# Attention block on one core: loads in cycles of 16 units, the remainder rows of P transposed by DMA

## The chip, the cores and the metric

The kernel runs on one core of a Trainium2 chip. Its time is the device time of that core in microseconds (us), the median over executions. The core has a matrix engine (TensorE, PE in the profile, with its weight loads shown apart as PEld), a vector engine (DVE), a scalar engine (ACT), GpSimd (POOL) and SyncE (SP), which computes nothing and issues transfers. Each engine works through its own list of instructions in order; semaphores tie the lists together. Sixteen DMA engines move the data.

## What is computed

Two independent attention blocks, A and B, have the same shapes: 16 batches, 144 query rows, model width 448, 16 heads, 512 keys, head width 256, all in bf16. K and V come from a cache. Each block is

```python
q = (x @ wq).reshape(B, Sq, H, Dh).transpose(0, 2, 1, 3)
scores = einsum("bhqd,bhkd->bhqk", q, k_cache) * (Dh ** -0.5)
p = softmax(scores, axis=-1)
o = einsum("bhqk,bhkd->bhqd", p, v_cache)
out = o.transpose(0, 2, 1, 3).reshape(B, Sq, H * Dh) @ wo
```

and the output joins A's and B's along the last axis.

## The kernel before

A **unit** U is one head of one batch: 256 units for A, then 256 for B. One Python loop over a step number i writes out the work of all engines in order; at step i it emits stages of several units at once, so that each engine always has work of some unit. `LQ`, `LS`, `LT` and `LSB` say how many steps a stage runs ahead of the step in which the unit's last stage, PV, is emitted.

- **Q** (L314, unit i+15): 8 matmuls project x of the unit's batch into one PSUM bank; `t_evac_q` (L326 on DVE or L330 on ACT) copies the result, scaled, to `qt_sb`.
- **SA** (L418, unit i+5): scores of the first 112 query rows, 2 matmuls of 512 columns into one of two banks. DVE takes the row maxima (L429), ACT the exponentials and their sums (L440), DVE the reciprocal (L450), POOL multiplies (L458, `t_norm`). The reciprocal and the multiplication of unit i+4 are emitted in step i, behind the maximum of unit i+5.
- **TA** (L471, unit i+2): four TensorE transposes of that P into the same bank; DVE copies them to `pt_sb` (L481).
- **SB, TB**: the remaining 32 query rows of four units share one set of 128 partitions. Every eighth step SB (L342) makes these scores for eight units in two banks; L354, L364, L374 and L382 do the softmax as above; TB (L394, four TensorE transposes for a group G of four units) and a DVE copy (L403, `t_evac_ptb`) bring them into the last 32 columns of `pt_sb`. TB stands between TA and PV in its step.
- **PV** (L504, unit i): 8 matmuls of V with the transposed P; ACT copies the result to `ring` (L519, L521).
- **OP** (L542): the product with wo, for chunks of 128 output rows, in pieces of two matmuls of 448 columns. A credit that grows by `OP_RATE` a step says how many pieces a step takes; a step takes none, one, two or more pairs. L560 evacuates a chunk, L571 stores it, issued on POOL.

A small planner (`_Sched`) puts in the semaphore waits: an instruction waits for the last writers of what it reads and the last readers of what it overwrites, and for nothing else.

SP issues the loads, in the order of `dma_plan`. K comes for eight units at a time through a transposing DMA of 2 MB (L290, three buffers), V for four units in a plain 1 MB copy (L299, three buffers), x for four batches in two transposing DMAs (L280, L281), the weights wq and wo as plain copies (L259, L261, L269). The list is sorted by the step in which the data is needed, so that a K and two V's alternate. A load whose buffer is still being read makes SP wait, and all later loads with it.

Of the kernel before, what the change touches and what calls it, by code (L numbers as in the profile page):

```python
# [122 lines left out]
def bass_concat_heads__mha_block_cached__gqa_block_cached__near_ridge_kernel(  # L123
# [37 lines left out]
    LQ, LS, LT = 15, 5, 2  # L161
    LSB = 7
    NK, NV, NXG = 3, 3, 3
    XB = 4 if Bn % 4 == 0 else (2 if Bn % 2 == 0 else 1)
    NQT, NPA, NPB, NPT, NST, NSTB, NOST = 12, 5, 2, 8, 4, 2, 3
# [9 lines left out]
    with contextlib.ExitStack() as es:  # L175
# [9 lines left out]
        kt_sb = sb("kt_sb", [128, NK, 2, 8 * SK], BF16)  # L185
# [4 lines left out]
        pb_sb = sb("pb_sb", [128, NPB, SK], BF16)  # L190
        pt_sb = sb("pt_sb", [128, NPT, 4, SQ], BF16)
        ost_sb = sb("ost_sb", [128, NOST, D], BF16)
        ident = sb("ident", [128, 128], BF16)
        ones = sb("ones", [128, 128], BF16)
# [7 lines left out]
        ptb_ps = [t.bitcast(BF16) for t in sb_ps]  # L202
# [3 lines left out]
        for i in range(NK):  # L206
            sem_names.append("kt%d" % i)
        for i in range(NV):
            sem_names.append("v%d" % i)
        for i in range(NXG):  # L210
            sem_names.append("xt%d" % i)
        for i in range(HG):
            sem_names.append("wq%d" % i)
        for i in range(NWG):
            sem_names.append("wo%d" % i)
        for i in range(NOST):
            sem_names.append("ost%d" % i)
        sems = {n: es.enter_context(nc.semaphore("s_" + n)) for n in sem_names}
# [10 lines left out]
        def t_ident():  # L229
            def e1(g):  # L230
                return g.memset(ones[:], 1.0)
            S.add(POOL, e1, writes=[("ones", 0)], name="ones")

            def e2(g):
                return g.affine_select(ident[:], ones[:], pattern=[[1, 128]], compare_op=ALU.is_equal,
                                       fill=0.0, base=0, channel_multiplier=-1)
            S.add(POOL, e2, reads=[("ones", 0)], writes=[("ident", 0)], name="ident")
# [36 lines left out]
        def t_load_x(XG):  # L274
            pr, j = divmod(XG, Bn // XB)
            sl = XG % NXG
            x = xs[pr][j * XB:(j + 1) * XB].rearrange("b q d -> (b q) d")

            def e(q):
                q.dma_start_transpose(xt_sb[:, sl, 0:3, :], x[:, 0:384]).then_inc(sems["xt%d" % sl], 16)  # L280
                return q.dma_start_transpose(xt_sb[:, sl, 3, :], x[:, 320:448]).then_inc(sems["xt%d" % sl], 16)  # L281
            S.add(SP, e, writes=[(("xt", sl), XG)], dma_sem="xt%d" % sl, n_dma=2, name="x%d" % XG)

        def t_load_k(SG):
            pr, r0 = divmod(8 * SG, NU)
            sl = SG % NK
            src = ks[pr].rearrange("b h k d -> (b h k) d")[r0 * SK:(r0 + 8) * SK, :]

            def e(q):
                return q.dma_start_transpose(kt_sb[:, sl, :, :], src).then_inc(sems["kt%d" % sl], 16)  # L290
            S.add(SP, e, writes=[(("kt", sl), SG)], dma_sem="kt%d" % sl, name="k%d" % SG)

# [9 lines left out]
        def t_q(U):  # L302
# [15 lines left out]
            S.add(PE, e, reads=[(("wq", hg), pr), ("wqz", 0), (("xt", xsl), XG)], writes=[("qp", ("q", U))],  # L318
                  banks=["qp"], name="Q%d" % U)

        def t_evac_q(U):
            sl = U % NQT
            src = qp_ps[:, 0:2 * SQ].rearrange("p (c q) -> p c q", c=2)
            if (U - LQ) % 8 in (2, 4, 6, 7):
# [8 lines left out]
        def t_sb(SG):  # L333
            ksl = SG % NK

            def e(t):
                ins = None
                for dc in range(2):
                    for jj in range(8):
# [3 lines left out]
                                       rhs=kt_sb[:, ksl, dc, jj * SK:(jj + 1) * SK], start=(dc == 0), stop=(dc == 1),  # L343
                                       tile_position=(0, 32 * j))
                return ins
            S.add(PE, e, reads=[(("qt", (8 * SG + jj) % NQT), 8 * SG + jj) for jj in range(8)] + [(("kt", ksl), SG)],
# [12 lines left out]
        def t_exp_b(G):  # L359
            sl = G % NSTB  # L360
            psl = G % NPB

            def e(a):
                return a.activation(pb_sb[:, psl, :], sb_ps[G % 2][:, :], AF.Exp,  # L364
# [3 lines left out]
                  writes=[(("pb", psl), (G, 0)), (("rsumb", sl), G)], banks=["sb%d" % (G % 2)], name="exb%d" % G)  # L368
# [8 lines left out]
        def t_norm_b(G):  # L377
            sl = G % NSTB
            psl = G % NPB

            def e(g):
                return g.tensor_tensor(pb_sb[:, psl, :], pb_sb[:, psl, :],  # L382
                                       stat[:, RINVB + sl:RINVB + sl + 1].to_broadcast([128, SK]), op=ALU.mult)
            S.add(POOL, e, reads=[(("pb", psl), (G, 0)), (("rinvb", sl), G)], writes=[(("pb", psl), (G, 1))],
                  name="nmb%d" % G)

        def t_tb(G):
            psl = G % NPB

            def e(t):  # L390
                src = pb_sb[:, psl, :].rearrange("q (p c) -> q c p", c=4)
                ins = None
                for c in range(4):
                    ins = t.transpose(ptb_ps[G % 2][:, c * 128:(c + 1) * 128], src[:, c, :], ident[:, :])  # L394
                return ins
            S.add(PE, e, reads=[(("pb", psl), (G, 1)), ("ident", 0)], writes=[(("sbb", G % 2), ("t", G))],
                  banks=["sb%d" % (G % 2)], name="TB%d" % G)

        def t_evac_ptb(G):
            s0 = (4 * G) % NPT  # L400

            def e(v):
                return v.tensor_copy(pt_sb[:, s0:s0 + 4, :, QA:SQ],  # L403
                                     ptb_ps[G % 2][:, 0:512].rearrange("p (c j q) -> p j c q", c=4, j=4))
            S.add(DVE, e, reads=[(("sbb", G % 2), ("t", G))],
                  writes=[(("ptb", (4 * G + j) % NPT), 4 * G + j) for j in range(4)], banks=["sb%d" % (G % 2)],
                  name="eptb%d" % G)

        def t_sa(U):
            SG = U // 8  # L410
            ksl = SG % NK
            bank = U % 2
            ko = (U % 8) * SK
# [7 lines left out]
            S.add(PE, e, reads=[(("qt", U % NQT), U), (("kt", ksl), SG)], writes=[(("sap", bank), ("s", U))],  # L421
# [144 lines left out]
        def t_store(r):  # L566
# [6 lines left out]
            S.add(POOL, e, reads=[(("ost", sl), r)], dma_sem="ost%d" % sl, name="st%d" % r)  # L573
# [4 lines left out]
        t_ident()  # L578
        dma_plan = []

        def plan(lo, deadline, lead, fn, *args):
            dma_plan.append((deadline, len(dma_plan), lo, lead, fn, args))

        s_min = -LQ - 24
        for XG in range(NXGT):
            pr, j = divmod(XG, Bn // XB)
            u_first = pr * NU + j * XB * H
            dl = u_first - LQ
            if XG >= NXG:
                pr0, j0 = divmod(XG - NXG, Bn // XB)  # L590
                lo = pr0 * NU + (j0 + 1) * XB * H - 1 - LQ + 1
            else:
                lo = s_min
            plan(lo, dl, 40, t_load_x, XG)
        for pr in range(NP):
            for hg in range(HG):
                dl = pr * NU + 4 * hg - LQ
                lo = pr * NU - H + 4 * hg + 3 - LQ + 1 if pr > 0 else s_min
                plan(lo, dl, 10 ** 6, t_load_wq, pr, hg)
        for wg in range(NWG):  # L600
            plan(s_min, H - 4 + 2 * wg, 10 ** 6, t_load_wo, 0, wg)
        for SG in range(NSG):
            dl = 8 * SG - LSB
            lo = 8 * (SG - NK) + 7 - LS + 1 if SG >= NK else s_min
            plan(lo, dl, 12, t_load_k, SG)
        for G in range(NG):
# [194 lines left out]
```

## Time and profile before

| what | us |
|---|---|
| median of 3 runs (lowest to highest) | 1213.86 (1212.51 to 1214.36) |
| span of the profiled execution | 1210.9 |
| DVE busy | 770.1 |
| ACT busy | 753.9 |
| POOL busy | 679.6 |
| TB, L394 MATMUL, 512 of them, busy | 49.8 |
| DVE copies behind TB, L403, 128 of them, busy | 53.0 |
| POOL multiplications L458 and L382, 640 of them, busy | 665.8 |
| store issues on POOL, L571, 36 of them, busy | 21.0 |

The span goes from the first to the last instruction of one profiled execution; a timed run holds some 3 us more. Busy time of PE is the sum of modelled matmul durations, and matmuls overlap, so PE's load is better read from the distance between the starts of matmuls of neighbouring steps. DMA moved 243 GB/s on the mean over the span.

### The profile page before, as it was taken

The numbers are of one execution on the slowest core, as the hardware profiler recorded it, in microseconds if no ns is written. First come the engines' busy times: TensorE is split into PE (matmuls) and PEld (weight loads), VectorE is DVE, ScalarE is ACT, GpSimd is POOL, SyncE is SP. The second block draws the span as 40 slices with busy tenths as digits, with TensorE's granted clock in tenths as the row PEclk, the third lists the DMA queues.
The fourth block names the chain that finished last, engine by engine and source line by source line (L and its number), as shares of the span: only waits on it lengthen the run. The fifth ranks groups of instructions, "written<-read, shape, count | busy, mean of one in ns | idle before, by whom it ended". The sixth has DMA issues, their size and how long they took to land.

```text
span 1210.9 us, 33868 instructions
## 1 busy us (share of the span) xinstructions
PE 1176.6 (97%) x13952; PEld 902.6 (75%) x13952; DVE 770.1 (64%) x2179; ACT 753.9 (62%) x2213; POOL 679.6 (56%) x682
## 2 busy tenths in 40 slices
PE   4998999999999999999999999999999999999997
PEld 3676777777777777777777777777877777777765
DVE  1765666666666666666566666666666666666563
ACT  1655666666666666666566666666666666666553
POOL 0654565565555565565555655655655655655553
PEclk9999999999999999999999999999999999999999
DMA  9999999999999999999999999999999999999971
GB/s 250 296 269 290 246 255 225 242 251 246 245 238 234 228 263 231 239 239 233 278 284 272 278 272 267 247 257 224 245 245 236 226 245 244 244 239 243 223 178 47
DMA packets 627033, 294.15 MB, mean 243 GB/s; under 512 B 548416, under 2 KB 556608, under 8 KB 626880
## 3 DMA queue, kind: packets, MB, share of 16 engines
q1 hardware_dynamic: 625152, 287.85, 102.2%
q0 software_dynamic: 1728, 4.13, 1.2%
q8 instruction: 111, 1.82, 0.6%
q14 instruction: 42, 0.34, 0.1%
HBM read 148.90 MB, written 4.13 MB: 126 GB/s over the span
## 4 chain that ended last, share of the span: by engine, by line
PE 90%; DMA 6%; DVE 2%; SPq 1%; ACT 0%; issue 0%; POOL 0%; ACTq 0%
PE qp_ps L314 20%; PE ot_ps L504 19%; PE sa_ps L418 18%; PE op_ps L542 17%; PE sa_ps L471 8%; PE sb_ps L342 5%; DMA kt_sb<-in_A_k_cache_dram 4%; PE sb_ps L394 2%; DMA kt_sb<-in_B_k_cache_dram 1%; DVE stat L429 1%; DMA wq_sb<-in_A_wq_dram 0%; PE qp_ps L542 0%; SPq L280 0%; DVE qt_sb L326 0%; DVE pt_sb L481 0%
## 5 line engine op out<-in xcount | busy, mean ns | idle before, releaser
L458 POOL TENSOR_TENSOR pa_sb<-pa_sb,stat 112x512 bf16<-112x512 bf16 x512 | 532.7, 1041 | 491.6 <-DVE stat L450 491.4
L440 ACT ACTIVATE pa_sb<-sa_ps,stat 112x512 bf16<-112x512 f32 x512 | 352.0, 688 | 409.6 <-DVE stat L429 408.6
L429 DVE TENSOR_REDUCE stat<-sa_ps 112x1 f32<-112x512 f32 x512 | 353.9, 691 | 324.7 <-PE sa_ps L418 321.4
L314 PEld LDWEIGHTS qp_ps<-xt_sb,wq_sb 128*128 128x128 bf16 x4096 | 290.5, 99 | 93.1 <-issue 11.3
L314 PE MATMUL qp_ps<-xt_sb,wq_sb 128*128 128x144 bf16 x4096 | 344.1, 228 | 16.1 <-DMA wq_sb<-in_A_wq_dram 10.3
L504 PE MATMUL ot_ps<-pt_sb,v_sb 128*128 128x144 bf16 x4096 | 340.9, 226 | 0.0
L418 PE MATMUL sa_ps<-kt_sb,qt_sb 128*112 128x512 bf16 x1024 | 311.1, 385 | 1.0 <-DVE pt_sb L481 0.8
L542 PE MATMUL op_ps<-wo_sb,ring 128*128 128x448 bf16 x1120 | 279.6, 353 | 0.0
L504 PEld LDWEIGHTS ot_ps<-pt_sb,v_sb 128*128 128x128 bf16 x4096 | 269.1, 98 | 0.4
L471 PEld LDWEIGHTS sa_ps<-ident,pa_sb 112*128 112x128 bf16 x2048 | 161.2, 114 | 104.9 <-ACT pa_sb L440 24.8
L519 ACT ACTIVATE ring<-ot_ps 128x288 bf16<-128x288 f32 (+8 forms) x512 | 190.3, 372 | 4.5 <-PE ot_ps L504 4.5
L481 DVE COPY pt_sb<-sa_ps 128x448 bf16<-128x448 bf16 x512 | 190.5, 372 | 2.4 <-PE sa_ps L471 2.4
L471 PE MATMUL sa_ps<-ident,pa_sb 112*128 112x112 bf16 x2048 | 186.5, 213 | 0.1
L326 DVE TENSOR_SCALAR qt_sb<-qp_ps 128x288 bf16<-128x288 f32 x256 | 117.0, 457 | 98.2 <-PE qp_ps L314 97.5
L382 POOL TENSOR_TENSOR pb_sb<-pb_sb,stat 128x512 bf16<-128x512 bf16 x128 | 133.1, 1040 | 27.1 <-DVE stat L374 27.1
L330 ACT ACTIVATE qt_sb<-qp_ps 128x288 bf16<-128x288 f32 x256 | 106.0, 414 | 35.1 <-PE qp_ps L314 33.4
L418 PEld LDWEIGHTS sa_ps<-kt_sb,qt_sb 128*112 128x112 bf16 x1024 | 96.9, 129 | 38.5 <-issue 26.8
L542 PEld LDWEIGHTS op_ps<-wo_sb,ring 128*128 128x128 bf16 x1120 | 95.5, 98 | 28.1 <-issue 0.9
L440 ACT ACTIVATION_READ_ACCUMULATOR pa_sb<-sa_ps,stat 112x1 f32 x512 | 98.9, 193 | 0.0
L354 DVE TENSOR_REDUCE stat<-sb_ps 128x1 f32<-128x512 f32 x128 | 87.1, 680 | 3.6 <-PE sb_ps L342 3.6
L364 ACT ACTIVATE pb_sb<-sb_ps,stat 128x512 bf16<-128x512 f32 x128 | 88.5, 691 | 0.0
L450 DVE RECIPROCAL stat<-stat 112x1 f32<-112x1 f32 x512 | 78.4, 153 | 0.5 <-ACT pa_sb L440 0.5
(23 smaller groups left out, 368.4 us busy)
## 6 DMA issues: line engine op xcount, KB each, us to landing
v_sb<-in_A_v_cache_dram SPq DMA_DIRECT2D x64, 1024.0 KB, 6.0
v_sb<-in_B_v_cache_dram SPq DMA_DIRECT2D x64, 1024.0 KB, 6.1
out_dram<-ost_sb POOLq DMA_DIRECT2D x36, 112.0 KB, 5.1
wo_sb<-in_A_wo_dram SPq DMA_DIRECT2D x8, 448.0 KB, 7.4
wo_sb<-in_B_wo_dram SPq DMA_DIRECT2D x8, 448.0 KB, 5.7
wq_sb<-in_A_wq_dram SPq DMA_DIRECT2D x4, 768.0 KB, 6.2
wq_sb<-in_B_wq_dram SPq DMA_DIRECT2D x4, 768.0 KB, 7.8
wq_sb<-in_A_wq_dram SPq DMA_DIRECT2D x4, 128.0 KB, 6.6
```

The lines of the kernel that those rows point to most:

```text
L314: ins = t.matmul(qp_ps[:, dc * SQ:(dc + 1) * SQ], lhsT=wq_sb[:, kc, c0:c0 + 128], rhs=xt_sb[:, xsl, kc, xo:xo + SQ], start=(kc == 0 and dc ...
L326: return v.tensor_scalar(qt_sb[:, sl, :, :], src, 1.0 / 16.0, None, op0=ALU.mult)
L382: return g.tensor_tensor(pb_sb[:, psl, :], pb_sb[:, psl, :], stat[:, RINVB + sl:RINVB + sl + 1].to_broadcast([128, SK]), op=ALU.mult)
L418: ins = t.matmul(sa_ps[bank][0:QA, :], lhsT=qt_sb[:, U % NQT, dc, 0:QA], rhs=kt_sb[:, ksl, dc, ko:ko + SK], start=(dc == 0), stop=(dc == 1))
L429: return v.tensor_reduce(stat[0:QA, NEG + sl:NEG + sl + 1], sa_ps[bank][0:QA, :], axis=AX.X, op=ALU.max, negate=True)
L440: return a.activation(pa_sb[0:QA, psl, :], sa_ps[bank][0:QA, :], AF.Exp, bias=stat[0:QA, NEG + sl:NEG + sl + 1], scale=1.0, accum_out=stat ...
L458: return g.tensor_tensor(pa_sb[0:QA, psl, :], pa_sb[0:QA, psl, :], stat[0:QA, RINV + sl:RINV + sl + 1].to_broadcast([QA, SK]), op=ALU.mult)
L471: ins = t.transpose(pta_ps[bank][:, c * 128:c * 128 + QA], src[:, c, :], ident[0:QA, 0:QA])
L481: return v.tensor_copy(pt_sb[:, sl, :, 0:QA], pta_ps[bank][:, 0:512].rearrange("p (c q) -> p c q", c=4)[:, :, 0:QA])
L504: ins = t.matmul(ot_ps[ob][:, dc * SQ:(dc + 1) * SQ], lhsT=v_sb[:, vsl, j, c * DH + dc * 128:c * DH + (dc + 1) * 128], rhs=pt_sb[:, sl, c, ...
L519: ins = a.activation(ring[:, 2 * h:2 * h + 2, c0:c0 + n1], src[:, :, 0:n1], AF.Copy)
L542: ins = t.matmul(acc[0:m, 0:D], lhsT=ring[:, c, col0:col0 + m], rhs=wo_sb[:, c, :], start=(c == first), stop=(c == last))
```

## The change

K comes in halves: one transposing DMA for four units (1 MB), four buffers. x comes for two batches at a time, the very first batch by itself. V has five buffers instead of three. The loads' places are written out by hand in cycles of 16 units; with T the first unit of a cycle they are, by step: T-4 (x and) the P transpose of eight units, T-3 two K halves, T+2 a K half and the second P transpose, T+4 a K half, T+5 three V's, T+8 one V, T+9 to T+11 the stores, which SP issues now. wo and wq have fixed steps too.

TB and its evacuation go. In their place a DMA on SP transposes the 32 remainder rows' P of eight units from SBUF to SBUF (`t_ptb_dma`, 256 KB), and a POOL copy for each group of four units (`t_copy_ptb`) puts them into `pt_sb`. The first copy of a pair is emitted in step T-1 (and T+7) behind that step's multiplication on POOL and just ahead of PV of unit T (T+8), which reads it; the second two steps later, two steps ahead of its reader.

Q runs 22, SA 13 and SB 14 steps ahead of PV instead of 15, 5 and 7; `pa_sb` has 13 buffers instead of 5. The exponential of the remainder rows writes its output in the order that the transpose wants. The first output chunks of A and B wait until steps 22 and 26, and `OP_RATE` grows by 10/9.

```diff
-    LQ, LS, LT = 15, 5, 2
-    LSB = 7
-    NK, NV, NXG = 3, 3, 3
-    XB = 4 if Bn % 4 == 0 else (2 if Bn % 2 == 0 else 1)
-    NQT, NPA, NPB, NPT, NST, NSTB, NOST = 12, 5, 2, 8, 4, 2, 3
+    LQ, LS, LT = 22, 13, 2
+    LSB = 14
+    NKH, NV, NXG = 4, 5, 2
+    WO_AT = ((10, 21), (21, 25))
+    OP_FROM = (22, 26)
+    XB = 2
+    NQT, NPA, NPB, NPT, NST, NSTB, NOST = 12, 13, 2, 8, 4, 2, 3
+    NPBT = 1
...
-            if (U - LQ) % 8 in (2, 4, 6, 7):
+            if (U - LQ + LSB) % 8 in (1, 3, 5, 6):
...
-                return a.activation(pb_sb[:, psl, :], sb_ps[G % 2][:, :], AF.Exp,
+                return a.activation(pb_sb[:, psl, G % 2, :], sb_ps[G % 2][:, :].rearrange("q (p c) -> q c p", c=4), AF.Exp,
...
-        def t_tb(G):
...
-        def t_evac_ptb(G):
...
+        def t_ptb_dma(SG):
+            psl = SG % NPB
+            tsl = SG % NPBT
+
+            def e(q):
+                return q.dma_start_transpose(pbt_sb[:, tsl, :, :, :].rearrange("p g c q -> p (g c) q"),
+                                             pb_sb[:, psl, :, :].rearrange("p g k -> p (g k)")).then_inc(
+                    sems["pb%d" % tsl], 16)
+            S.add(SP, e, reads=[(("pb", psl, g), (2 * SG + g, 1)) for g in range(2)], writes=[(("pbt", tsl), SG)],
+                  dma_sem="pb%d" % tsl, name="pb%d" % SG)
+
+        def t_copy_ptb(G):
+            tsl = (G // 2) % NPBT
             s0 = (4 * G) % NPT
...
+            def e(g):
+                return g.tensor_copy(pt_sb[:, s0:s0 + 4, :, QA:SQ],
+                                     pbt_sb[:, tsl, G % 2, :, :].rearrange("p c (j q) -> p j c q", j=4))
+            S.add(POOL, e, reads=[(("pbt", tsl), G // 2)], writes=[(("ptb", s0 + j), 4 * G + j) for j in range(4)],
+                  name="cptb%d" % G)
...
-            S.add(POOL, e, reads=[(("ost", sl), r)], dma_sem="ost%d" % sl, name="st%d" % r)
+            S.add(SP, e, reads=[(("ost", sl), r)], dma_sem="ost%d" % sl, name="st%d" % r)
...
+        plan(s_min, s_min, -LQ, t_load_x_first)
+        for hg in range(HG):
+            plan(s_min + (1 if hg < 2 else 3), s_min, 4 * hg - LQ, t_load_wq, 0, hg)
+        for KH in range(2):
+            plan_k(s_min + 2, KH)
+        plan(s_min + 4, s_min, H - LQ, t_load_x, 0)
+        for KH in range(2, 4):
+            plan_k(s_min + 5, KH)
+        plan_v(s_min + 6, 0)
+        plan_v(s_min + 6, 1)
+        plan_v(-5, 2)
...
+        for n in range(0, NSG, 2):
+            t = 8 * n
+            XG = (t + 32) // (XB * H)
+            if (t + 32) % (XB * H) == 0 and XG < NXGT:
+                plan(t - 4, (XG - 1) * XB * H - LQ, XG * XB * H - LQ, t_load_x, XG)
+            plan_pb(t - 4, n)
+            if n + 2 < NSG:
+                plan_k(t - 3, 2 * n + 4)
+                plan_k(t - 3, 2 * n + 5)
+                plan_k(t + 2, 2 * n + 6)
+            plan_pb(t + 2, n + 1)
+            if n + 2 < NSG:
+                plan_k(t + 4, 2 * n + 7)
+            for j, at in enumerate((5, 5, 5, 8)):
+                if 2 * n + 3 + j < NG:
+                    plan_v(t + at, 2 * n + 3 + j)
...
-        OP_RATE = float(NCH * NWO) / NU
+        OP_RATE = 10.0 / 9 * NCH * NWO / NU
...
-            while stores and stores[0][1] <= i:
+            while stores and stores[0][1] <= i and (i % 16 in (9, 10, 11) or i >= NT - 4):
...
-            if ok and ph == 3:
-                t_tb(ga)
-                t_evac_ptb(ga)
-            if ok and ph == 7:
-                t_tb(gb)
-                t_evac_ptb(gb)
...
+            if i % 8 == 7 and 0 <= i + 1 < NT:
+                t_copy_ptb((i + 1) // 4)
+            if i % 8 == 1 and 0 <= i < NT:
+                t_copy_ptb((i + 3) // 4)
```

## The prediction

> **What bounds the kernel now.** I read the busy shares and the chain first, then single steps in the timeline, then the DMA engines.
>
> ```profile
> PE 1176.6 (97%) x13952; PEld 902.6 (75%) x13952; DVE 770.1 (64%) x2179; ACT 753.9 (62%) x2213; POOL 679.6 (56%) x682
> ...
> PE 90%; DMA 6%; DVE 2%; SPq 1%; ACT 0%; issue 0%; POOL 0%; ACTq 0%
> ```
>
> PE is busy throughout and the chain runs over PE; the other engines have a third of their time free. As PE's busy time is modelled, I check it against starts in PE's timeline of three neighbouring steps:
>
> ```profile
> 561.66 0.59 PE L418 MATMUL sa_ps<-kt_sb,qt_sb 128*112 128x512 bf16 x2
> 562.10 0.36 PE L471 MATMUL sa_ps<-ident,pa_sb 112*128 112x112 bf16 x4
> 562.29 0.67 PE L504 MATMUL ot_ps<-pt_sb,v_sb 128*128 128x144 bf16 x8
> ...
> 563.67 0.59 PE L418 MATMUL sa_ps<-kt_sb,qt_sb 128*112 128x512 bf16 x2
> 564.11 0.36 PE L471 MATMUL sa_ps<-ident,pa_sb 112*128 112x112 bf16 x4
> 564.30 0.39 PE L394 MATMUL sb_ps<-ident,pb_sb 128*128 128x128 bf16 x4
> 564.53 0.66 PE L504 MATMUL ot_ps<-pt_sb,v_sb 128*128 128x144 bf16 x8
> ```
>
> A step with one OP pair lasts 2.01 us (561.66 to 563.67) and no matmul waits in it; starts are closer than durations, so the array is fed without a hole. TB shifts PV by 0.23 us (564.53 instead of 564.30). So what leaves PE is gained, and what makes PE wait is lost, to the full amount. The exception are steps without an OP pair: there consecutive SA start 1.78 us apart though PE has only 1.63 us of work; the next TA waits for the exponential:
>
> ```profile
> PEld sa_ps L471 <- ACT pa_sb L440: 24.8, 88, 0.6
> ```
>
> The loads stand just behind PE. In half microseconds of the stretch 400 to 420 us:
>
> ```profile
> GB/s 0 0 57 98 262 319 414 356 246 292 229 168 199 2 9 135 292 288 292 289 290 291 288 292 289 291 290 289 167 53 172 332 385 401 414 197 53 12 82 53
> ```
>
> A plain copy (V) runs at about 400 GB/s, a transposing one (K) at 290, with troughs at each change of kind. Eight units take 18.03 us in the steady part; a K of 2.1 MB at 290 and two V's at 390 need 7.2 + 5.4 = 12.6 us of them. The rest, 5.4 us, is troughs and SP's waits for a free V buffer:
>
> ```profile
> SPq L299 <- PE op_ps L542: 235.3, 59, 12.8
> ```
>
> PE's waits for K sum to only some 9 us, most of them before 130 us. Regrouping the loads therefore frees room on the DMA engines, which is not what bounds; a gain has to come from PE.
>
> **The sum, part by part**, against the span of 1210.9.
>
> (a) TB off PE: 128 groups. By starts, a TB costs 0.23 us in a step with OP work (106 of them) and 0.14 in a step without (22; consecutive SA 1.92 apart instead of 1.78): 23.9 + 3.1 = 27.0 us off. DVE's 53 us at L403 and POOL's 21 us of store issues go too; neither engine bounds, so they count nothing.
>
> (b) The new credit. Counting the rule by hand over 512 steps, 102 were without an OP pair and 130 will be (chunks drain faster, then wait for the next batch); each such step holds 0.15 us that PE can't use: 28 x 0.15 = 4.2 us on.
>
> (c) The POOL copy. This is the term that decides. The first copy of each pair is emitted behind the multiplication of its step and read by the very next PV. What POOL is paced by stands in the same stretch:
>
> ```profile
> 562.29 0.69 DVE L429 TENSOR_REDUCE stat<-sa_ps 112x1 f32<-112x512 f32 x1
> 562.90 0.15 DVE L450 RECIPROCAL stat<-stat 112x1 f32<-112x1 f32 x1
> ...
> 563.14 1.04 POOL L458 TENSOR_TENSOR pa_sb<-pa_sb,stat 112x512 bf16<-112x512 bf16 x1 [0.97 <-DVE stat L450]
> ```
>
> The reciprocal stands behind the maximum of the following SA, so the multiplication starts 0.85 us after a PV begins and ends at 564.18; the next PV would begin, without TB, at 564.30. The longer lead of SA does not change this: it moves the units, not the order within a step. So the copy begins where PV wants its result. With a copy of C and some 0.05 us for the semaphore, PV waits C - 0.07 us in a step with one OP pair.
> C is in no row. POOL's one-column memsets take 0.10 us, L231 fills 128 columns in 0.205, so 0.83 ns a column: 512 columns give 0.52 us, the low end. L235, one input and one output, takes 0.294 for 128: 1.5 ns a column, 0.88 us. The multiplication with two inputs, 1.04, is the far end.
>
> ```profile
> L235 POOL TENSOR_SCALAR_AFFINE_SELECT ident<-ones 128x128 bf16<-128x128 bf16 x1 | 0.3, 294 | 0.1
> L231 POOL MEMSET ones<- 128x128 bf16 x1 | 0.2, 205 | 0.3 <-POOLq L786 0.3
> ```
>
> I take 0.65, a copy having less to compute than the select. There are 64 such places (every eighth step). The credit count puts no OP pair into 23 of these steps, one into 33, two into 4, three into 4. One pair: 0.58 us. None: PV would come 0.23 us earlier, so 0.81, but the next TA's 0.15 us wait is spent meanwhile: 0.66. Two pairs: 0.20; three: nothing. 23 x 0.66 + 33 x 0.58 + 4 x 0.20 = 35 us on. With C = 0.52 it is 27, with 0.88 it is 49, with 1.04 it is 59. The second copy of a pair has two steps in hand and costs nothing; without that cover it would cost the same again. Multiplications behind a copy are late by C, but their TA is now ten steps away. A gain is excluded: nothing in POOL's order gets shorter.
> The Trainium skill speaks against this move: "GPSIMD Engine Reference", section 3.1, calls ordinary elementwise work better placed on DVE and gives 769 ns for a tight loop over 512 elements, while its section 4.1 calls one-input work roughly line-rate. By 769 ns term (c) would be an estimated 42 us. L235's row lies near the first statement, and no row shows a POOL copy.
>
> (d) The P transposes by DMA: 64 of 256 KB, SBUF to SBUF, in no row. At K's 290 GB/s each moves in 0.9 us, the low end; the dearest nearer row is x's first DMA (L280, 432 KB), up to 3.54 us on SP, and L281 (144 KB) takes 2.08. I take 2.1. Behind each on SP's queue stand the K halves. In SP's order the first K halves of a cycle start about step T-5 and land near T-1.5, needed by SB at T+2: 3.5 steps, over 7 us, cover two transposes at 2.1. POOL's copy waits for the transpose as well and POOL's multiplications behind it; it lands near T-5 and the copy is emitted at T-1. The same cover holds for the stores on SP (36, at 0.4 to 0.6 us, emitted after their evacuation). So nothing on, and up to the second rival if the cover is gone.
> The Trainium skill, "VectorE: DVE Perf Modes", section on the three transpose paths, has 390 ns for a 128x128 transpose on TensorE and 1309 ns by DMA. Eight such blocks in a row would be an estimated 10.5 us for each DMA, 21 us a cycle, and would decide for the second rival. K's row (2.1 MB, 64 such blocks, in 7.2 us of movement) speaks against taking them one after another.
>
> (e) The beginning. First Q at 10.3 now; with x of one batch it comes some 0.8 us earlier, since the two x issues took 2.9 us and wq stands behind them. The first PV moves from 37.9 to about 50: eight Q's at 1.66 us apart, an SB, 14 steps of Q and SA at about 1.75. Of the 12 us, 8.0 are work that is merely done earlier (7 Q, 8 SA, one SB). Net 4 on; the early waits for K, 6.0 us before 130 us, I take as gone: 2 off. Bounds: 8 off to 10 on, as K's second pair lands just when SB wants it.
>
> (f) At the change from A to B PE loses 5.4 us around 585 to 600 (K, x and wq together); spread out, 4 off. (g) The end: Q and SA stop earlier, leaving 7 steps without Q and OP, held at about 1.5 us by the SA-exponential-TA chain against 1.1 of work: 2.8 on. The last store took 4.9 us after its issue on POOL; on SP, where unloaded copies land sooner, 1.7 off. Together 1 on.
>
> Sum: -27.0 + 4.2 + 35 - 2 - 4 + 1 = +7, span 1218. The median of the runs lies 2.9 us above the span: **1221 us**.
>
> **Rivals.** *First, PV does not wait for the copy* (a copy far below every row, or a multiplication that comes earlier than today): (c) falls to 0, 1183 + 3 = 1186; with C = 0.3, 1199. For it speaks POOL's 44% idle time; against it the order on POOL, which puts that idle time ahead of the multiplication, not behind it. Faster needs C below about 0.47.
> *Second, the loads become the bound.* A cycle of 16 units moves K 14.5, V 10.8, P transposes 1.8, x and stores 0.9: 28 us. PE's cycle is 35.2 us plus two waits of 0.55: 36.3. If the troughs go with the changes of kind, one set of 5.4 us makes 33.4, and it fits. If every transfer keeps its own, two sets make 38.8: 2.5 us x 31 cycles = 78 us on, 1298; halfway 40, 1260. It decides once loads and troughs pass 36.3 us. For it: troughs also occur within a K; the K halves at T+2 and T+4 may start only when SA has left their buffers. Against: half as many changes of kind, and five V buffers end SP's 235 us of waits.
> *Third, the regrouping does nothing and the beginning is longer than I think*: (e) at its upper bound, 1231; inside my range.
>
> **How the numbers follow.** Chances: my forecast, with C between 0.5 and 0.9, 0.60, alone 1206 to 1236; first rival 0.23; second 0.12; third 0.05. Left below 1185 is a third of the first rival (0.08), above 1250 most of the second (0.09), hence the range 1185 to 1250. A measurement can tell 0.2%, 2.4 us, from no change. Faster: the first rival and the low edge of the forecast, 0.33; the same (1211.4 to 1216.3): 0.13; slower: 0.54.
>
> **What would show it.** The wait view should have PV waiting for POOL some 55 to 60 times at about 0.6 us, and PE's starts should have no TB. The copy's row gives C at once. Right or wrong for (d): the time to landing of the P transposes and PE's waits for K after 130 us. The forecast is wrong if PV waits for the copy under 0.3 us, or if SB waits for K in every cycle.

## The result and the profile after

The changed kernel takes 1255.74 us (median of four runs, 1251.83 to 1255.99) against 1214.11 for the kernel before in the same series (1212.51 to 1216.04): ratio 1.0338 [1.0319, 1.0357], 42 us more. The prediction was 1221, with a range of 1185 to 1250. The direction was right, the size was not: the time lies 6 us outside the range. The span of the profiled execution grew from 1210.9 to 1254.2 us. (One execution's time lies 1.7 us above its own span, as 1255.94 and 1254.2 here; the 3 us named at the top set the median against one execution's span.) The page of the changed kernel, its busy shares, the granted clock in 40 slices, the chain and the costliest group with a wait:

```profile
PE 1175.2 (94%) x13440; PEld 881.6 (70%) x13440; DVE 732.0 (58%) x2051; ACT 750.4 (60%) x2213; POOL 727.9 (58%) x774
...
PEclk9898999999999999999899989999999999999999
...
PE 73%; POOL 7%; DVE 7%; issue 5%; DMA 4%; SPq 3%; ACT 1%; DVEq 0%
...
L521 PE MATMUL ot_ps<-pt_sb,v_sb 128*128 128x144 bf16 x4096 | 344.5, 227 | 29.1 <-POOL pt_sb L421 29.1
```

512 PE instructions fewer, and yet PE's share of the chain fell from 90% to 73%. POOL, absent from the chain before (0%), has 7%. PE's busy time hardly moved, though TB's 49.8 us are gone; a slower clock, which stretches the matmuls that are left, is one reason: four slices of the clock now show an 8. What PE waits for (total us, times, longest us):

```profile
PE ot_ps L521 <- POOL pt_sb L421: 29.1, 57, 3.1
PE sb_ps L359 <- DMA kt_sb<-in_A_k_cache_dram: 12.0, 4, 5.1
...
PE qp_ps L333 <- issue: 8.5, 1, 8.5
...
PE sb_ps L359 <- DMA kt_sb<-in_B_k_cache_dram: 3.4, 1, 3.4
```

The first row is the wait for the POOL copy, spread evenly but for three places. The others are a handful of long holes. Where they lie, the stretches of the changed kernel show (window, its length, busy time and count of PE, PEld, DVE, ACT and POOL, granted clock, DMA share, GB/s):

```profile
0.00:150.00 150.00, 113.61 (x1188) 82.11 (x1189) 72.21 (x197) 70.86 (x196) 69.48 (x78) 0.94 1.12 252
150.00:575.00 425.00, 416.05 (x4878) 315.64 (x4877) 264.97 (x747) 271.91 (x807) 264.60 (x280) 1.00 1.10 255
575.00:625.00 50.00, 40.06 (x449) 29.47 (x446) 24.95 (x71) 26.07 (x87) 24.99 (x27) 0.90 1.13 273
625.00:725.00 100.00, 98.13 (x1148) 74.13 (x1145) 61.03 (x172) 62.72 (x186) 60.05 (x65) 1.00 1.10 265
725.00:750.00 25.00, 18.99 (x185) 13.88 (x183) 9.53 (x28) 10.26 (x33) 10.55 (x12) 0.83 1.18 255
```

and of the kernel before:

```profile
0.00:150.00 150.00, 126.34 (x1473) 94.33 (x1474) 84.33 (x234) 79.83 (x223) 70.73 (x75) 1.00 1.14 269
...
575.00:625.00 50.00, 47.21 (x555) 36.11 (x554) 30.00 (x86) 30.05 (x88) 27.78 (x28) 0.97 1.16 279
...
725.00:750.00 25.00, 25.00 (x302) 19.63 (x300) 16.59 (x48) 16.51 (x46) 15.90 (x16) 1.00 1.18 268
```

Three stretches lost PE time and clock together: the beginning, the change from A to B, and the place where B's wo is loaded. In the two long even stretches PE keeps its full clock and all but some 2% of the time.

**Where the 43 us of span come from.** For the accounts below I counted PE's idle time from starts: the distance between two matmul starts, less the shortest distance that the shape shows in both traces (0.216 us for SA's 512 columns, 0.064 for SB's, 0.063 for 144, 0.189 for 448, 0.056 for TB's 128, 0.049 for 112). A slower clock counts as idle time in this: by the same count some 9 us of the changed kernel's idle time (an estimate) are work that ran at half clock, and 1.5 us of the idle time before. The work itself fell from 1149.3 to 1120.7 us (TB, 28.6), the idle time between matmuls rose from 44.5 to 121.5, the first matmul comes 1.4 us earlier and the end lies 3.6 us closer to the last one: -28.6 + 77.0 - 1.4 - 3.6 = 43.4. Of the 77, 38.8 stand between TA and PV: 7.5 in three places where the copy itself came late, behind the P transpose, and 31.3 elsewhere, nearly all of it in the order on POOL. Of the other 38, 16 stand in the beginning, 6 at the change, 7 between 700 and 750, and 8 elsewhere, 4 of these behind 1200; the table in the next section has the stretches, TA to PV included, beside the experiments.

The change from A to B, in the timeline of the changed kernel (start, duration, engine and line, in brackets the idle time before it):

```profile
594.59 0.50 SPq L267 DMA_DIRECT2D wq_sb<-in_B_wq_dram  x1
595.14 0.51 SPq L269 DMA_DIRECT2D wq_sb<-in_B_wq_dram  x1
...
598.49 0.54 PE L559 MATMUL op_ps<-wo_sb,ring 128*128 128x448 bf16 x2
598.65 0.61 SPq L267 DMA_DIRECT2D wq_sb<-in_B_wq_dram  x1
...
601.25 7.39 SPq L410 DMA_TRANSPOSE pbt_sb<-pb_sb  x1
607.46 0.61 PEld L333 LDWEIGHTS qp_ps<-xt_sb,wq_sb 128*128 128x128 bf16 x6 [8.88 <-issue]
```

The two pieces of B's first wq group are issued at 594.59 and 595.14, and Q of unit 256 stands next on PE from 599 on. By the trace the second piece lands at 607.40, 12.3 us after its issue, and that Q starts at 607.49. The wait view calls this hole "issue"; what ends it is the landing of wq, and in the run without that load (e9, below) the hole is gone. SP then holds the next P transpose for 7.39 us behind it. And in the beginning, the two holes around 50 to 62 us, one for the P transpose (through the copy), one for K:

```profile
53.80 1.14 PE L521 MATMUL ot_ps<-pt_sb,v_sb 128*128 128x144 bf16 x8 [3.07 <-POOL pt_sb L421]
61.94 1.45 PE L359 MATMUL sb_ps<-kt_sb,qt_sb 128*32 128x512 bf16 x16 [2.88 <-DMA kt_sb<-in_A_k_cache_dram]
```

Eight PV matmuls that take some 0.67 us elsewhere take 1.14 here: the clock records have half the clock for 6.8 us from 52.2, and for 37.6 us in all up to the last matmul (3.4 before).

### The profile page after: what moved, and what is told of

The parts are those of the page before. It is cut to its first block, busy times and chain, and to the rows that moved or that the text cites. A ratio compares the mean times of both kernels' runs of the same rounds, so it can differ in the third digit from the quotient of the medians.

```text
span 1254.2 us, 32874 instructions
## 1 busy us (share of the span) xinstructions
PE 1175.2 (94%) x13440; PEld 881.6 (70%) x13440; DVE 732.0 (58%) x2051; ACT 750.4 (60%) x2213; POOL 727.9 (58%) x774
## 4 chain that ended last, share of the span: by engine, by line
PE 73%; POOL 7%; DVE 7%; issue 5%; DMA 4%; SPq 3%; ACT 1%; DVEq 0%
PE ot_ps L521 17%; PE op_ps L559 16%; PE qp_ps L333 15%; PE sa_ps L435 14%; PE sa_ps L488 5%; PE sb_ps L359 5%; POOL pa_sb L475 5%; POOL pt_sb L421 3%; DMA kt_sb<-in_A_k_cache_dram 2%; DVE qt_sb L345 2%; SPq L309 2%; DVE stat L446 2%; DMA pbt_sb<-pb_sb 2%; DVE stat L467 1%; DVE pt_sb L498 1%
## 5 line engine op out<-in xcount | busy, mean ns | idle before, releaser
L475 POOL TENSOR_TENSOR pa_sb<-pa_sb,stat 112x512 bf16<-112x512 bf16 x512 | 532.1, 1039 | 469.5 <-DVE stat L467 467.9
L333 PE MATMUL qp_ps<-xt_sb,wq_sb 128*128 128x144 bf16 x4096 | 347.8, 229 | 26.2 <-DMA wq_sb<-in_A_wq_dram 9.4
L521 PE MATMUL ot_ps<-pt_sb,v_sb 128*128 128x144 bf16 x4096 | 344.5, 227 | 29.1 <-POOL pt_sb L421 29.1
L435 PE MATMUL sa_ps<-kt_sb,qt_sb 128*112 128x512 bf16 x1024 | 315.0, 390 | 4.5 <-DVE pt_sb L498 3.1
L559 PE MATMUL op_ps<-wo_sb,ring 128*128 128x448 bf16 x1120 | 275.5, 354 | 0.0
L400 POOL TENSOR_TENSOR pb_sb<-pb_sb,stat 128x512 bf16<-128x512 bf16 x128 | 133.0, 1039 | 27.7 <-DVE stat L392 27.7
L359 PE MATMUL sb_ps<-kt_sb,qt_sb 128*32 128x512 bf16 x1024 | 70.8, 399 | 15.9 <-DMA kt_sb<-in_A_k_cache_dram 12.0
```

The lines of the kernel that those rows point to most:

```text
L333: ins = t.matmul(qp_ps[:, dc * SQ:(dc + 1) * SQ], lhsT=wq_sb[:, kc, c0:c0 + 128], rhs=xt_sb[:, xsl, kc, xo:xo + SQ], start=(kc == 0 and dc ...
L359: ins = t.matmul(sb_ps[jj // 4][32 * j:32 * j + 32, :], lhsT=qt_sb[:, U % NQT, dc, QA:SQ], rhs=kt_sb[:, (U // 4) % NKH, dc, j * SK:(j + 1) ...
L435: ins = t.matmul(sa_ps[bank][0:QA, :], lhsT=qt_sb[:, U % NQT, dc, 0:QA], rhs=kt_sb[:, ksl, dc, ko:ko + SK], start=(dc == 0), stop=(dc == 1))
L475: return g.tensor_tensor(pa_sb[0:QA, psl, :], pa_sb[0:QA, psl, :], stat[0:QA, RINV + sl:RINV + sl + 1].to_broadcast([QA, SK]), op=ALU.mult)
L521: ins = t.matmul(ot_ps[ob][:, dc * SQ:(dc + 1) * SQ], lhsT=v_sb[:, vsl, j, c * DH + dc * 128:c * DH + (dc + 1) * 128], rhs=pt_sb[:, sl, c, ...
L559: ins = t.matmul(acc[0:m, 0:D], lhsT=ring[:, c, col0:col0 + m], rhs=wo_sb[:, c, :], start=(c == first), stop=(c == last))
```

## The experiments

Ratios are to the kernel before on the same chip, intervals 95%. "Hole" means several us without a matmul.

| run | what | median us | ratio |
|---|---|---|---|
| e1_copy_first | first copy ahead of the multiplication | 1232.05 | 1.0169 [1.0150, 1.0188] |
| e2_weights | B's weights earlier and later | 1250.43 | 1.0312 [1.0285, 1.0339] |
| e3_start | V's and x behind K at the start | 1254.27 | 1.0337 [1.0321, 1.0354] |
| e4_tb_back | TB back on PE, loads stay regrouped | 1213.74 | 1.0000 [0.9986, 1.0014] |
| e6_k_ahead | e1 + one K half ahead of the P transpose | 1234.39 | 1.0170 [1.0149, 1.0190] |
| e7_all | e6 + e2 + e3 | 1233.12 | 1.0165 [1.0136, 1.0194] |
| e7c_wo5 | e7 + A's first wo at step 5 | 1234.99 | 1.0160 [1.0124, 1.0196] |
| e8_no_p_dma | e1 without the P transposes | 1217.61 | 1.0035 [1.0022, 1.0048] |
| e9_no_reload | e1 without B's weights | 1211.61 | 0.9980 [0.9966, 0.9994] |
| e10_half_v | e1 with half of each V | 1209.70 | 0.9968 [0.9952, 0.9984] |
| e11_long | before + 4 waits of 7 us | 1253.04 | 1.0312 [1.0296, 1.0329] |
| e12_short | before + 16 waits of 1.8 us | 1239.50 | 1.0205 [1.0182, 1.0228] |
| e13_lead11 | e4 with SA 11 steps ahead | 1220.91 | 1.0054 [1.0042, 1.0066] |
| e14_lead11_wo | e13 + A's first wo at step 5 | 1220.16 | 1.0043 [1.0028, 1.0058] |

PE's idle time by stretch, us, counted as above from each run's trace:

| stretch | before | after | e1 | e4 | e8 | e9 | e10 |
|---|---|---|---|---|---|---|---|
| 0 to 150 | 25.3 | 47.6 | 45.4 | 32.2 | 39.6 | 48.6 | 37.8 |
| 575 to 625 | 5.4 | 13.7 | 12.6 | 0.9 | 10.7 | 1.0 | 7.1 |
| 700 to 750 | 0.4 | 10.7 | 8.3 | 3.4 | 8.3 | 0.3 | 4.4 |
| the rest | 13.4 | 49.5 | 28.6 | 16.5 | 24.4 | 28.3 | 24.1 |

**e1_copy_first: is it the copy's place?**

```diff
+            if i % 8 == 7 and 0 <= i + 1 < NT:
+                t_copy_ptb((i + 1) // 4)
             u = i + LS
...
-            if i % 8 == 7 and 0 <= i + 1 < NT:
-                t_copy_ptb((i + 1) // 4)
```

> Only the first POOL copy of each pair moves: it is emitted ahead of its step's multiplication instead of behind it. Theory 1 (the copy behind the multiplication holds PV up, 29 to 37 us in 57 waits): those waits go, 1222 to 1229 us. Theory 2 (the loads are the bound: K lands only 0.1 to 4 us ahead of every second SB, so a faster PE waits for K instead): 1245 us or more, with the lost waits found again at SB for K.

24 us came off; the time is 3 us above what the first theory had. The waits:

```profile
PE sb_ps L359 <- DMA kt_sb<-in_A_k_cache_dram: 16.9, 8, 5.9
...
PE ot_ps L521 <- POOL pt_sb L421: 7.3, 3, 3.1
```

The copy costs nothing any more except in the three places where the transposed P itself is late. But PE, now faster, waits for A's K 16.9 us in 8 places instead of 12.0 in 4: the idle time between TA and PV fell by 31 us, the time by 24, so part of the gain went into other waits. A cycle of 16 units takes 35.28 us in the even part (36.35 in the changed kernel, 36.07 before). The kernel still stands 18 us above the one before, so the copy is not all.

**e4_tb_back: is it the regrouping?** TB and its DVE copy return, the P transposes and POOL copies go; K halves, five V buffers and the cycles of 16 units stay.

```diff
-    LQ, LS, LT = 22, 13, 2
-    LSB = 14
+    LQ, LS, LT = 15, 13, 2
+    LSB = 7
...
-            plan_pb(t - 4, n)
-            plan_pb(t + 2, n + 1)
-            plan((8, 9, 10, 12)[hg] + NU - 32, lo, dl, t_load_wq, 1, hg)
+            plan((8, 9, 13, 17)[hg] + NU - 32, lo, dl, t_load_wq, 1, hg)
...
+            if ok and ph == 3:
+                t_tb(ga)
+                t_evac_ptb(ga)
```

> The regrouped loads alone: TB on PE and its DVE copy are back, no P transpose by DMA and no POOL copy; Q and SB lead by 15 and 7 again, SA still by 13. Theory 1 (regrouping neither gains nor costs in the steady part; TB costs 27 us, the copy's waits of 33 us go, the late loads at the start and at A to B stay): 1235 to 1250 us, 36.1 us for 16 units in the steady part. Theory 2 (the regrouped loads with their K halves waiting for buffers are what costs): 1260 us or more. Theory 3 (P by DMA is what costs, regrouping is fine): 1215 us or less.

The time of the kernel before, within 0.14%, over ten runs. As a whole the regrouped loads are neither gain nor loss. Stretch by stretch they are both: the table has 6.9 us more idle time at the start, 3.0 and 3.1 more in 700 to 750 and in the rest, 4.5 less at the change, and behind the last matmul, where the stores now come from SP, 3.6 us are gained. (The traced execution took 1217.44 us.) The same two windows at the change from A to B, of e4:

```profile
590.00:600.00 10.00, 9.96 (x120) 7.13 (x118) 6.55 (x20) 6.16 (x19) 4.49 (x5) 1.00 1.25 177
600.00:610.00 10.00, 10.00 (x121) 8.05 (x119) 6.56 (x19) 6.44 (x19) 6.87 (x7) 1.00 1.15 291
```

and of the changed kernel:

```profile
590.00:600.00 10.00, 8.71 (x99) 6.65 (x97) 5.26 (x16) 6.20 (x22) 6.77 (x8) 1.00 1.04 381
600.00:610.00 10.00, 2.51 (x24) 1.30 (x24) 0.00 (x0) 0.41 (x1) 0.42 (x1) 0.59 1.28 322
```

In e4 the hole is not there. With Q 15 steps ahead, the first wq of B, loaded at step 232, has 9 steps to the step that needs it; with Q 22 ahead it has 2. So the 42 us come with the transposition of P by DMA and POOL and with the longer leads of Q and SB (e4 undoes both and keeps SA's 13). That does not clear the loads: the next runs keep both, and win time back by loading less.

**e8_no_p_dma, e9_no_reload, e10_half_v: do the loads have room?** All three start from e1 and take transfers away.

```diff
# e8
-            plan_pb(t - 4, n)
-            plan_pb(t + 2, n + 1)
# e9
-        for pr in range(NP):
+        for pr in range(1):
             for wg in range(NWG):
...
-            plan((8, 9, 10, 12)[hg] + NU - 32, lo, dl, t_load_wq, 1, hg)
# e10
+                if G >= NV:
+                    return q.dma_start(v_sb[:, sl, 0:2, :], src[:, 0:2, :]).then_inc(sems["v%d" % sl], 16)
```

> The kernel with the copy ahead of the multiplication, without the 64 P transposes by DMA: pbt is set to zero once, so the 32 remainder rows of each unit are left out of PV; POOL's copies, leads and all other loads stay. Theory A (the loads of a cycle fill its 35 us, the P transposes took the last room and K lands late behind them): K lands 3 us or more ahead of every SB in the steady part, most of the waits at the start and at A to B go, 1198 to 1212 us. Theory B (K is late because its half buffers come free only 8 steps before SB wants them, whatever else is loaded): 1225 us or more, K still 0.1 to 2 us ahead.

> The kernel with the copy ahead of the multiplication, without the loads of B's wq and wo (B is computed with A's weights). It prices the change of weights: theory A (7.3 MB in cycles without room land on PE and cost half clock besides): the waits near 589 and 722 to 731 us go, 1232 falls by 18 to 26 us, to 1206 to 1214. Theory B (PE is held there by something else, K or the P transposes): 1222 us or more.

> The kernel with the copy ahead of the multiplication; from the sixth V on, only half of each V is loaded (the other half of the units uses old V): 5.4 us of copies less in each cycle, nothing else. Theory A (bytes): the waits for K and P from 60 us on shrink to under a third, 1195 to 1212 us. Theory B (buffers): 1225 us or more, K's lead over every second SB unchanged.

Against e1: 14.4, 20.4 and 22.3 us off. e9 and e10 came out in the ranges of their first theories; e8 fell between its two numbers. The gains overlap and must not be added. The table tells where each acts. Without B's weights the two holes of B vanish (12.6 to 1.0, 8.3 to 0.3) and the start gains nothing. Without the P transposes the cycle in the even part stays at 35.29 us, as in e1: there they are free. What goes is 5.8 us in the start, 1.9 at the change and 4.2 in the rest (12 us of span, 14.4 between the medians). Of these, 7.7 us lie between TA and PV: they are PV's waits for the late P itself. PE's waits for K hardly fall, from 20.0 us in e1 (A's and B's) to 18.3:

```profile
PE sb_ps L359 <- DMA kt_sb<-in_A_k_cache_dram: 12.7, 4, 6.6
...
PE sb_ps L359 <- DMA kt_sb<-in_B_k_cache_dram: 5.6, 1, 5.6
```

How far K is ahead can be read from the landing times in the traces. For every second SB the later of its two K halves lands, behind the first four cycles, 0.1 to 2.9 us ahead of SB in e1 and 1.8 to 5.4 us in e8 (0.1 in one place, B's wo): the P transposes take some 2 us of a thin cover, less than the 3 us or more for every SB that the first theory had. With half of V's bytes PE's idle time shrinks in all four stretches and vanishes in none. The waits of e10 for A's K:

```profile
PE sb_ps L361 <- DMA kt_sb<-in_A_k_cache_dram: 9.0, 4, 3.2
```

9.0 us in 4 places against e1's 16.9 in 8. From 60 us on the waits for K and P fall from 24.7 to 9.7 us, not quite to the third that was expected. So the loads are not the bound of the even part, but have so little room that less in the queue at a crowded place shows on PE at once.

**e2_weights, e3_start, e6_k_ahead, e7_all, e7c_wo5: is it only the order of the loads?** Each moves loads and removes no byte.

```diff
# e2
-    WO_AT = ((10, 21), (21, 25))
-    OP_FROM = (22, 26)
+    WO_AT = ((10, 21), (21, 37))
+    OP_FROM = (22, 34)
-            plan((8, 9, 10, 12)[hg] + NU - 32, lo, dl, t_load_wq, 1, hg)
+            plan((4, 4, 6, 10)[hg] + NU - 32, lo, dl, t_load_wq, 1, hg)
# e3
-        plan_v(s_min + 6, 1)
-        plan_v(-5, 2)
+        plan_v(-2, 1)
+        plan_v(-2, 2)
-                plan(t - 4, (XG - 1) * XB * H - LQ, XG * XB * H - LQ, t_load_x, XG)
+                plan(t + 2 if n == 0 else t - 4, (XG - 1) * XB * H - LQ, XG * XB * H - LQ, t_load_x, XG)
# e6 (on e1)
+                plan_k(t - 4, 2 * n + 4)
             plan_pb(t - 4, n)
-                plan_k(t - 3, 2 * n + 4)
# e7c (on e7)
-    WO_AT = ((10, 21), (21, 37))
+    WO_AT = ((5, 21), (21, 37))
```

> Only the places of the weight loads at the change from A to B: wq's first two groups before the V's of their cycle, the last four wo groups 12 steps later, OP of B from step 34. Theory 1 (these 7 MB don't fit behind the copies of a cycle; PE waits 8.5 us for Q, some 6 us around 735 us, and the granted clock is 0.5 for 10.2 + 10.2 us after these waits): 1231 to 1239 us, no 8 us hole, no half clock after 590 us. Theory 2 (the DMA engines have no room anywhere, the hole only moves): 1250 us or more.

> Only the order of the first loads: V for units 4 to 11 and x for batches 2 and 3 go behind the first P transpose and two K halves. Theory 1 (PV 0 waits 3.1 us for its P transpose, the third SB 2.9 us for K, because these copies and x stand ahead of them on SP; half clock follows): both waits shrink, 1244 to 1250 us. Theory 2 (the start is bound by bytes, order does nothing): 1254 to 1257 us.

> On top of the copy ahead of the multiplication: in SP's list the first K half of each cycle changes places with the P transpose ahead of it. Theory 1 (K lands late because that P transpose waits, at the head of SP's list, for the POOL copy to free its only buffer, some 3 us, with K behind it): K of every second SB lands 3 to 5 us ahead instead of 0.1 to 2, fewer waits of SB for K and fewer spells of half clock, 1216 to 1225 us. Theory 2 (K is late because of the bytes before it): 1229 us or more.

> All edits together: copy ahead of the multiplication, K half ahead of the P transpose, the weight loads at A to B and the first loads as in the two kernels before. Theory 1: the moved weights, which gained 5 us alone, gain more where K has room: 1198 to 1212 us, steady part 35.3 us for 16 units. Theory 2: 1225 us or more.

> As the kernel before it, and the first four wo groups of A at step 5 instead of step 10, ahead of three V's instead of right ahead of the P transpose and K. Theory 1: the wait of SB for K near 95 us (5 to 6 us, then 6.8 us of half clock) shrinks, 4 to 8 us under the kernel before it. Theory 2 (bytes): within 2 us of it.

e2 gained 5 us, hardly more than the noise, where the first theory had 17 or more: the hole at 599 went and one of 3.9 us for PV came at 616; the one behind wo stayed. e3 gained nothing: the waits at 50 and 58 us went, and PV waited 4.7 us at 86. e6 put K ahead of the P transpose, and PV waited for the P transpose 7 to 8 us at 49, 89 and 725 instead. e7, with all of it, is where e1 is, 1233.12 against 1232.05, and I had expected 1212 or less; its largest holes are for PV, 11.1 us at 83 and 8.9 at 599. e7c moved 2 us, within its spread. None of the five orders gained more than e2's 5 us: in e2, e3, e6 and e7 a load that came earlier made another late.

**e13_lead11, e14_lead11_wo: can e4 be made faster through K?** e4's waits for K, 12.9 us in 4 places, looked like a shorter SA lead could free K's buffers sooner.

```diff
# e13 (on e4)
-    LQ, LS, LT = 15, 13, 2
+    LQ, LS, LT = 15, 11, 2
-                plan_k(t + 4, 2 * n + 7)
+                plan_k(t + 5, 2 * n + 7)
# e14 (on e13)
-    WO_AT = ((10, 21), (21, 25))
+    WO_AT = ((5, 21), (21, 25))
```

> The kernel with regrouped loads and TB back on PE, with SA 11 steps ahead instead of 13 (the last K half of a cycle one step later, since its buffer is then free two steps later): the same bytes in the same order, K wanted two steps later. Theory A (in the first 100 us and at the wo loads K lands late against what the lead of SA asks for; less lead gives it time): the waits of SA for K at 14, 31, 50 and 86 us (13.7 us together) fall to under 7, 1203 to 1210 us, faster than both kernels. Theory B (bytes alone set the start): within 3 us of 1213.7.

> As the kernel before it, with the first four wo groups at step 5, ahead of three V's, instead of step 10, right ahead of two K halves. Theory A: the wait for K near 86 us goes or shrinks below 2 us, 2 to 6 us under the kernel before it. Theory B: the same within 2 us.

e13 is 7 us slower than e4, which neither theory had; e14 stays within a us of it. By starts the waits for K in the first 100 us fell from 13.7 to 8.5 us, not under 7, and a hole for V came instead. PE's timeline of e13:

```profile
115.06 1.14 PE L523 MATMUL ot_ps<-pt_sb,v_sb 128*128 128x144 bf16 x8 [6.88 <-DMA v_sb<-in_A_v_cache_dram]
```

In e14, whose wait for K near 86 us is gone as its first theory had it, the wait for V comes at 70.8 us with 8.07. No version that computes everything beats the kernel before.

**e11_long, e12_short: what does a hole cost beyond its length?** On the kernel before, PV waits for POOL memsets of 2048 columns, 16 of them in both: four at a time in four places, or one at a time in 16.

```diff
# e11; e12 has 16 units, one memset each
+            if i in (100, 180, 340, 420):
+                for j in range(4):
+                    S.add(POOL, lambda g: g.memset(idle[:], 0.0), writes=[("idle", (i, j))], name="idle%d.%d" % (i, j))
```

> The kernel before the change, with four long holes: at four units PV also waits for four POOL memsets of an idle tile (2048 columns each, about 1.8 us by 0.83 ns a column). What a wait of PE costs beyond itself. Theory A (a wait of several us is followed by a spell of half clock, as after the changed kernel's waits): PE waits 4 x 7.4 = 30 us, four spells of half clock of 6.8 to 10 us, 40 to 52 us over before. Theory B (the clock does not follow the waits): 26 to 33 us over before.

> The kernel before the change, with the same number of memsets spread out: at sixteen units PV also waits for one POOL memset of 2048 columns. Theory A (short waits leave the clock alone): 16 x 1.8 = 29 us of waits and no half clock after 100 us, 26 to 32 us over before, 12 to 20 us under the kernel with four long holes. Theory B: the same as that kernel.

e11 is 38.2 us slower than the kernel before in its series (1214.88), e12 24.6. PE's wait, the clock and a window of e11 with a hole in it:

```profile
PE ot_ps L505 <- POOL idle L688: 28.3, 4, 7.7
...
core 0: 1249.0 us, clock 0.984
...
272.00:280.00 8.00, 3.98 (x25) 3.06 (x26) 0.24 (x1) 0.82 (x2) 5.84 (x5) 0.50 0.24 90
280.00:288.00 8.00, 8.00 (x90) 6.45 (x89) 5.03 (x15) 4.08 (x11) 3.54 (x4) 0.90 0.15 35
```

and of e12, the two windows around a short hole with and one without a spell of half clock (holes of 2.3 and 1.4 us):

```profile
PE ot_ps L505 <- POOL idle L688: 22.1, 15, 2.1
...
core 0: 1236.5 us, clock 0.997
...
248.00:256.00 8.00, 5.89 (x58) 4.85 (x56) 4.04 (x13) 4.12 (x12) 6.15 (x7) 0.79 1.15 251
350.00:358.00 8.00, 6.72 (x87) 4.88 (x85) 3.62 (x12) 3.38 (x9) 4.07 (x4) 1.00 0.83 205
```

Four holes of 7 to 8 us give four spells of half clock, 10.2, 6.8, 6.8 and 6.8 us. The short holes (1.1 to 2.3 us by starts; one of the sixteen memsets made none) give one spell, 3.4 us, after one of the two longest. What a hole costs beyond its length comes from comparing the starts of PV, step by step, with the kernel before: the four long holes of 7.0, 7.0, 7.9 and 7.0 us cost 9.7, 8.4, 9.3 and 8.6 us, so 1.3 to 2.7 us each beyond the wait, 7.0 us together. That is half of what is left of each spell once the hole has ended. In e12 the one hole with a spell cost 1.4 us beyond its length, the other fourteen nothing. (The rest of e11's 37.8 us in the trace, some 2 us, stands in the start.) Both came in a little under the theory that the clock follows long waits: e11 at 38.2 where it had 40 or more, above the 33 at most of no effect; e12 at 24.6 where it had 26, 13.5 us under e11 as expected (12 to 20), but with one spell where none was forecast.

## Why the prediction was right in direction and wrong in size

Against the span of 1210.9 the prediction summed to +7, the measurement is +43.

- **(a) TB off PE, 27.0 off: right.** (106 x 0.23 is 24.4, so by its own numbers the term is 27.5.) The work fell by 28.6, and a cycle in the even part, with the copy out of the way, went from 36.07 us (before) to 35.28 (e1).
- **(c) The POOL copy, 35 on: right, and the mechanism with it.** It was put at 0.65 us and takes 0.610. PV waits for POOL 57 times (predicted 55 to 60) for 29.1 us in the wait view, which holds the three late transposes too; by starts the copy alone costs 31.3 us. The count of places was right, 23 without an OP pair and 33 with one, and PV waits 0.70 and 0.48 us there where P is not late (forecast 0.66 and 0.58), 0.10 with two pairs and nothing with more. In the kernel the copy is emitted ahead of PV of unit T-1; on POOL it starts when that PV has long begun, so that the PV it holds up is that of unit T, as the prediction said. Emitted ahead of the multiplication instead, 24 us of the time go (e1). The row of the copy:

```profile
L421 POOL COPY pt_sb<-pbt_sb 128x512 bf16<-128x512 bf16 x128 | 78.0, 610 | 12.3 <-PE ot_ps L521 6.8 <-DMA pbt_sb<-pb_sb 5.5
```

- **(d) The P transposes, "So nothing on": the first step that failed.** The cover failed, not the price: "3.5 steps, over 7 us" were to lie between the landing of the first K halves and SB, and in the changed kernel they land 0.1 to 4.2 us ahead. The price of a transpose was put too high, if anything. SP's issue of one and its way to landing (min/median/max):

```profile
L410 SPq DMA_TRANSPOSE pbt_sb<-pb_sb x64: 1231/1308/7386, 46.1 to 1225.1; - x64
...
DMA to landing us min/median/max: 3.0/4.2/12.3
```

1.31 us against the 2.1 assumed. And thin as the cover turned out, it holds in the even part, 35.28 us with them and 35.29 without. It does not hold where other loads share the queue: there P itself lands late, PV waits for it (7.7 us in e1), and taking the transposes out gives 14.4 us (e8). The cover was reckoned from the steady cycle alone. It overlooked too that a P transpose waits for POOL's copies out of the single `pbt_sb`, with the K halves queued behind it. SP waits longer still for the half buffers of K themselves (L309, 417 us in 93 waits), which only the second rival named. Of SP in the changed kernel, its waits and one of them:

```profile
SPq L410 <- POOL pt_sb L421: 132.1, 40, 13.4
...
447.24 0.51 SPq L588 DMA_DIRECT2D out_dram<-ost_sb  x1
453.37 1.24 SPq L410 DMA_TRANSPOSE pbt_sb<-pb_sb  x1
454.65 9.92 SPq L309 DMA_TRANSPOSE kt_sb<-in_A_k_cache_dram  x2
```

SP stands still for 5.6 us (447.75 to 453.37) with K halves next in line. A second buffer for `pbt_sb` should take that wait away; this was not tried. Its worth for K is in doubt: in e8, which has no such wait at all, PE's waits for K went from 20.0 to 18.3 us only.

The Trainium skill, "VectorE: DVE Perf Modes", section on the three transpose paths, gave 1309 ns for one 128x128 block by DMA, and by that an estimate of 10.5 us for each P transpose. The trace differs: eight blocks land 4.2 us after their issue. The prediction did not use the estimate.

- **(e) The beginning, "2 off": wrong by over 20 us.** PE idles 47.6 us before 150 us where the kernel before idled 25.3. (4.8 of it are late P transposes and 1.0 the copy's waits, which (d) and (c) count as well; without them the term is off by some 17.) The early waits for K, which I took as gone, are there (58.7, 96.1 and 139.0 us, 11.2 us together). With SB 14 and SA 13 steps ahead the same loads are wanted earlier. e3, e6 and e7 moved the holes about and left 43.9 to 48.4 us of idle time; only fewer transfers made it clearly smaller: 37.8 us with half of V (e10), and 39.6 without the P transposes (e8), where nearly all that goes is the wait for P itself.
- **(f) The change from A to B, "4 off": wrong, some 18 on** (575 to 625: 5.4 to 13.7; and 700 to 750, which I hadn't considered, 0.4 to 10.7). I put the loads of K, x and wq as spread out. With Q 22 steps ahead B's wq has 2 steps; without the reload 20.4 us go (e9).
- **(b) and (g)**, 4.2 and 1 on: of the right order at the end, 5.7 us idle between 1200 and 1225 against 3.6 gained behind the last matmul. For (b) the trace has the 130 steps without an OP pair as counted (102 before); what they cost was not measured apart.

The sentence behind (d), (e) and (f) is the one from the first view: that the regrouping "frees room on the DMA engines, which is not what bounds". e4 shows that the regrouping gained nothing, and e8 to e10 that what then stood in the queue had hardly any room left. The second rival (the loads become the bound, chance 0.12, 1260 to 1298) had the right resource and the wrong form: it lets the loads decide in every cycle, "once loads and troughs pass 36.3 us", and in the even part e1 runs at 35.28 with or without the P transposes. PE waits for loads in the three stretches that carry something extra, and the long holes there cost clock as well. Of the first rival, by the prediction's own terms C = 0.3 gives some 1201, not 1199; nothing rests on it. Still open: how much of the start's loss is bytes, and how much the shorter time for which half a K buffer is free; no run had a fifth K half.

## What to carry to other kernels

Reckon the room of a load queue at its crowded places (start, change of weights), not in the steady cycle: a small transfer that is free there can cost 14 us here, and a longer lead of a stage shortens the time that its weights have. An instruction whose reader comes next, placed behind a long one on an engine that a chain paces, costs most of its duration each time (here 31 of 64 x 0.61 us); place it in front of the paced one. When a hole moves instead of closing under several reorderings, leave a transfer out and see what that is worth, before trying another order.

## What the hardware showed that was not expected

- **A hole in PE costs clock.** Four holes of 7 to 8 us brought 6.8 to 10.2 us of half clock each, worth 1.3 to 2.7 us a hole beyond the wait, half of what was left of the spell when the hole ended; fifteen short holes brought a single spell of 3.4 us, worth 1.4 (e11, e12). In the changed kernel twelve holes of over 0.9 us go with 37.6 us of half clock.
- The Trainium skill, "TensorE: Matmul & The Clock Gate", Part 1, has the clock fall to half after an idle window of about 3.4 us, a window that runs freely. The spells here, 3.4, 6.8 and 10.2 us, are multiples of it; but one of two 2.3 us holes in e12 was enough for a spell, below the gap that the page warns of.
- **A POOL copy of 512 bf16 columns takes 610 ns**, 59% of a multiplication of the same width with two inputs (1039). A DMA that transposes 256 KB within SBUF takes 1.31 us on SP and 4.2 us to land (medians of 64).
